# Halved value steps behind a modelled instruction store, tables of rules per stretch, and bulk transfers in pieces, in a four-layer attention kernel

## The chip, the cores and the metric

The program runs on one core of a Trainium2 chip. A core has five engines that run side by side and meet only at semaphores: TensorE (PE, matmuls; its weight loads are shown apart as PEld), ScalarE (ACT), VectorE (DVE), GpSimd (POOL) and SyncE (SP, which here only issues transfers). The metric is the device time of one execution in microseconds (us), median of several runs.

## The reference

The input is 2048 tokens of 512 numbers, with 32 heads of 16. Four residual blocks follow each other: A, B, A, B, with the same weights in both A and in both B.

```python
def A(x, wqkv, wo):                       # softmax attention
    q, k, v = heads(x @ wqkv)
    p = softmax(einsum("bhqd,bhkd->bhqk", q, k) * 16 ** -0.5)
    return merge(einsum("bhqk,bhkd->bhqd", p, v)) @ wo

def B(x, wqkv, w_phi, wo):                # linear attention, learned feature map
    q, k, v = heads(x @ wqkv)
    phi = lambda t: concat(softmax(t @ w_phi), softmax(-t @ w_phi))
    kv, z = phi(k).T @ v, phi(k).sum(0)
    return merge(phi(q) @ kv / (phi(q) @ z + 1e-6)) @ wo

for block in (A, B, A, B):
    x = x + block(layernorm(x))
```

An A block needs 32 x 2048 x 2048 exponentials, and that is where most of the time lies.

## The kernel before

**Tiles.** An A block (class LayerA) works on 32 groups: a group G is four heads and 512 queries. Within a group it goes over 16 steps kt of 128 keys, and each step has two halves of 128 x 1024 scores. So a block has 32 x 16 x 2 = 1024 score tiles. Three things happen to a tile:

- a *score step* on TensorE (`scores`, `score_cols`, L1266): 8 loads of weights and 8 matmuls of 512 columns in 16-bit numbers, into one of two PSUM tiles `s`;
- the exponential on ScalarE (L1273), from `s` to one of six SBUF tiles `p`;
- a *value step* on TensorE (`pvs`, L1316), one for the two tiles of a step kt: 8 matmuls of 512 columns in the program, in 32-bit numbers. Each of these stands in the trace as two matmuls and two weight loads. They sum into an accumulator, a pair of PSUM banks named `double` or `pm`.

A few tiles do not go through ScalarE: for them `power_task` forms the exponential by a polynomial on VectorE (L1284 to L1304), from a score step into `double` or `pm` to the one tile `px`. They are called *power tiles* below.

**Fillers.** Between these steps TensorE gets the rest of the block as *filler steps*: the projections of the next heads and the output projection (`mm_cols`, L713, 8 matmuls of 512 columns in 16-bit numbers, the shape of a score step), the transposes at the end of a block (L1386), and in the first block the turns and folds of block B's weights (`prep_b`, L438 and L446). They come from generators that yield ("pe", planned time).

**What sets the order.** `attention` is a planner that runs when the program is built. It keeps a modelled time for TensorE (`pe`), ScalarE (`act`) and the other engines, and writes the instructions down in the order that it finds. The engines follow that order on the chip and wait for semaphores only. In each turn it takes a score step if one of the two `s` tiles is free by then (`free`, from the start of the exponential before the last one, plus BACK), else a filler or a value step, if it is planned to end by the time the next score step is due. A value step may run over that time by LATE = 0.2 us. The planned prices are UNIT 0.217 us for a score or filler step, STEP 0.864 for a value step, EXP 0.904 for an exponential, 0.66 for a turn, a fold or a group of transposes. EAGER sets from which step on power tiles are taken although a filler waits: never in the first A block, always in the second.

**Blocks B** follow their own planners (`feed`, `flow`), with the same tables before and after.

**Transfers.** All bulk transfers are issued on SP, in the order of the program: an instruction that waits for a semaphore holds back everything behind it. Weights of block B are prepared during the first A block and go through DRAM (`split_parts`, `load_hl`, `begin`), as do parts of the attention output (`load_ob`, L1324).

## Time and profile before

| | |
|---|---|
| median of 3 runs | 2498.81 us (2496.61, 2498.81, 2501.56) |
| the profiled execution | 2493.94 us, span 2492.2 us |
| granted TensorE clock, mean | 0.989 |
| ScalarE busy | 2136.6 us, 86% of the span |
| TensorE busy | 2303.5 us, 92% |
| exponentials on ScalarE (L1273) | 2001, from 71.0 to 1008.3 us and from 1311.7 to 2238.8 us |

The two stretches in the last row are the A blocks; blocks B and the preparation lie around them. Times in rows of the profile are us from the start of the span. In rows of a timeline the columns are start, duration, engine, source line, operation, output and inputs, shape, and the number of instructions merged into the row; in brackets stands idle time of the engine before it and what ended it. The lines L are those of the kernel before, except in rows that are said to be of the changed one.

### The profile page before, as it was taken

The numbers are of one execution on the slowest core, as the hardware profiler recorded it, in microseconds if no ns is written. First come the engines' busy times: TensorE is split into PE (matmuls) and PEld (weight loads), VectorE is DVE, ScalarE is ACT, GpSimd is POOL, SyncE is SP. The second block draws the span as 40 slices with busy tenths as digits, with TensorE's granted clock in tenths as the row PEclk, the third lists the DMA queues.
The fourth block names the chain that finished last, engine by engine and source line by source line (L and its number), as shares of the span: only waits on it lengthen the run. The fifth ranks groups of instructions, "written<-read, shape, count | busy, mean of one in ns | idle before, by whom it ended". The sixth has DMA issues, their size and how long they took to land.

```text
span 2492.2 us, 103433 instructions
## 1 busy us (share of the span) xinstructions
PE 2303.5 (92%) x46698; PEld 1083.9 (43%) x46698; DVE 1602.2 (64%) x2866; ACT 2136.6 (86%) x2379; POOL 530.6 (21%) x644
## 2 busy tenths in 40 slices
PE   6999999999989999899889999999999999998998
PEld 4444444444434443445344444444443444444543
DVE  8233456756667455889973666667567652469897
ACT  6899999999999999444539999999999999993553
POOL 3111111121110000356441112111111000005553
PEclk9999999999999999999899999999999999999999
DMA  5412240132045331100124004203300441120003
GB/s 195 69 27 44 49 82 20 43 48 50 3 104 126 118 112 62 52 35 18 61 72 77 19 7 63 34 3 51 65 4 15 88 128 48 66 70 26 26 1 112
DMA packets 114925, 142.86 MB, mean 57 GB/s; under 512 B 64184, under 2 KB 69928, under 8 KB 112168
## 3 DMA queue, kind: packets, MB, share of 16 engines
q1 hardware_dynamic: 113288, 133.38, 21.7%
q8 instruction: 367, 6.01, 1.0%
q0 software_dynamic: 1184, 2.77, 0.3%
q14 instruction: 86, 0.70, 0.1%
HBM read 62.16 MB, written 41.94 MB: 42 GB/s over the span
## 4 chain that ended last, share of the span: by engine, by line
ACT 58%; PE 14%; issue 12%; DVE 12%; POOL 2%; DMA 0%; ACTq 0%; POOLq 0%; SPq 0%; DVEq 0%
ACT p L1273 57%; PE double L1316 3%; PE s L1266 2%; DVE su L1691 1%; PE pbv L1618 1%; PE pk L1618 1%; PE pq L1618 1%; PE pm L713 1%; DVE yt L1908 1%; DVE f L1683 1%; POOL f L1700 1%; DVE f L1684 1%; PE fl L1950 1%; DVE mx L1680 1%; PE pm L1316 1%
## 5 line engine op out<-in xcount | busy, mean ns | idle before, releaser
L1273 ACT ACTIVATE p<-s 128x1024 f32<-128x1024 f32 x2001 | 1853.0, 1063 | 19.2 <-PE s L1266 15.2
L1266 PE MATMUL s<-kq 49*32 49x512 f16 x15136 | 789.7, 381 | 102.7 <-ACT p L1273 86.8
L1266 PEld LDWEIGHTS <-kq 49*32 49x32 f16 x15872 | 385.8, 89 | 881.8 <-issue 795.9
L1316 PE MATMUL double<-p,v 64*32 64x512 f32 x9064 | 612.7, 591 | 0.0
L1316 PE MATMUL pm<-p,v 64*32 64x512 f32 x6944 | 475.6, 589 | 0.0
L977 POOL TENSOR_TENSOR yt<-yt,yt 128x512 f32<-128x512 f32 x64 | 84.8, 1324 | 764.1 <-DVE yt L974 742.3
L1316 PEld LDWEIGHTS double<-p,v 64*32 64x32 f32 x9064 | 174.1, 106 | 30.9 <-issue 6.2
L1618 PEld LDWEIGHTS <-xnTa 128*128 128x128 f16 x1152 | 111.1, 99 | 155.1 <-DVE f L1684 26.4
L1350 DVE SCALAR_TENSOR_TENSOR xt<-pm,c_oA,xt 128x512 f32<-128x512 f32 x102 | 76.2, 747 | 155.9 <-PE pm L713 151.9
L1097 POOL TENSOR_TENSOR sq<-stg 128x512 bf16<-128x512 f16 x48 | 57.7, 1202 | 478.1 <-DVE stg L1005 250.6
L1316 PEld LDWEIGHTS pm<-p,v 64*32 64x32 f32 x6944 | 135.0, 106 | 21.6 <-issue 2.6
L1700 POOL TENSOR_TENSOR f<-f,su 128x1024 f32<-128x1024 f32 x58 | 112.2, 1934 | 116.3 <-DVE su L1694 103.4
L974 DVE STREAM_TRANSPOSE yt<-double 128x512 f32<-128x512 f32 x72 | 47.3, 695 | 112.3 <-PE double L1316 112.1
L1618 PE MATMUL pbv<-wbv,xnTa 128*128 128x512 f16 x384 | 93.9, 397 | 21.7 <-DVE f L1684 21.7
L1685 ACT ACTIVATE f<-f,c_pB 128x1024 f32<-128x1024 f32 x62 | 70.4, 1148 | 49.6 <-DVE f L1684 42.3
L1706 ACT ACTIVATE fk<-f 128x1024 f16<-128x1024 f32 x30 | 31.7, 1057 | 74.7 <-POOL f L1700 74.7
L713 PEld LDWEIGHTS <-wA 64*32 64x32 f16 x4608 | 75.9, 93 | 44.8 <-issue 9.2
L974 DVE STREAM_TRANSPOSE yt<-pm 128x512 f32<-128x512 f32 x56 | 36.8, 696 | 90.4 <-PE pm L1316 90.1
L1000 DVE TENSOR_SCALAR tq<-double,c_qk 128x512 f32<-128x512 f32 x28 | 21.0, 749 | 108.0 <-PE double L713 101.0
L1618 PE MATMUL pq<-wbqk,xnTa 128*128 128x512 f16 x384 | 88.4, 379 | 0.7 <-DVE vt L1645 0.7
L1618 PE MATMUL pk<-wbqk,xnTa 128*128 128x512 f16 x384 | 88.1, 379 | 0.0
L1950 PE MATMUL fl<-wbo,obB 128*128 128x512 f16 x312 | 76.7, 403 | 8.7 <-ACT raw L1902 3.6
(342 smaller groups left out, 3083.2 us busy)
## 6 DMA issues: line engine op xcount, KB each, us to landing
kq<-stg SPq DMA_DIRECT2D x168, 128.0 KB
xd<-xt SPq DMA_DIRECT2D x40, 512.0 KB
xt<-xd SPq DMA_DIRECT2D x40, 512.0 KB
v<-vyt SPq DMA_DIRECT2D x384, 16.0 KB
oD<-osp SPq DMA_DIRECT2D x24, 256.0 KB
ob<-oD SPq DMA_DIRECT2D x8, 768.0 KB
xt<-in_A_x_dram SPq DMA_DIRECT2D x8, 512.0 KB
wbqk<-dBqk SPq DMA_DIRECT2D x2, 2048.0 KB
```

The source lines that it names most:

```text
L713: nc.tensor.matmul(ps[h][c, :], w[r, c], x[r], start=(n == 0), stop=(n == of - 1), skip_group_check=True)
L974: nc.vector.transpose(ys[u].rearrange("p a b -> p (a b)"), ps[u])
L977: nc.gpsimd.tensor_tensor(ys[0], ys[0], ys[1], ALU.add)
L1097: nc.gpsimd.tensor_tensor(sq, hi, hi, ALU.mult)
L1266: nc.tensor.matmul(banks2[u][32 * c:32 * c + 32, :], self.side(g, half, 64 * u, 0, kt * P + 32 * c, 32), self.side(g, half, 64 * u, 1, j * ...
L1273: nc.scalar.activation(pt, s, AF.Exp, scale=EXPS)
L1316: nc.tensor.matmul(acc[h][32 * hh:32 * hh + 32, :], self.oct[o]["v"][r, x:x + 32], pt[r, hh % 2, :], start=(kt == 0), stop=(kt == NT - 1), ...
L1350: nc.vector.scalar_tensor_tensor(xt[:, u, :], ps[h], con["oA"], xt[:, u, :], op0=ALU.mult, op1=ALU.add)
L1618: nc.tensor.matmul(dst, xnT[:, a, c, t * P:(t + 1) * P], w(b, c), start=(i == 0 and c == 0), stop=(i == 2 and c == NC4 - 1))
L1685: nc.scalar.activation(f, f, AF.Exp, scale=con["pB"])
L1700: nc.gpsimd.tensor_tensor(f3, f3, self.part_sums(f3, slice(0, 64), factor), ALU.mult)
L1950: nc.tensor.matmul(ps2[:, u, :], obs[j][:, c, a, t * P:(t + 1) * P], wo[:, b, c, :], start=(c == 0 and i == 0), stop=(c == NC4 - 1 and i = ...
```

## The change

1. **Halves.** `pvs` can do the columns 0 to 255 or 256 to 511 alone. Where a whole value step does not fit the room before the next score step, the planner may issue the first half (planned price HALF = 0.434 us), and the second when that fits. A half has as many matmuls and weight loads as a whole step, each over half the columns.
2. **The gate.** A first half is taken only while a modelled store of TensorE's instructions is well filled (`line[1] >= LEVEL`). The store holds at most DEPTH = 300 instructions and fills at RATE = 60 per us. Each score or filler step takes 16 out of it and each value step, whole or half, 32. If the model runs empty, planned time passes.
3. **Tables.** RULES replaces EAGER and LATE. For each A block and each of 16 stretches of 32 steps it has three numbers: how readily power tiles are taken (0 never, 1 if no filler waits, 2 always), by how much a whole step or a second half may run over, and by how much a first half may.
4. **Prices.** A turn or a group of transposes is planned at 0.85 and a fold at 1.15 us (still fitted as 0.66), and an exponential that had to wait for its scores costs 0.016 more.
5. **Two conditions.** Tiles of a group whose keys are not loaded yet no longer hold back other steps, and a filler that wants a PSUM pair may take one before a new accumulator if both are free.
6. **Pieces.** `spread` issues a bulk transfer as several, each with a part of every partition's row: 8 for block B's query and key weights, 4 for 1 MB tables, 3 for a block of attention output, 2 for the value weights.

```diff
+HALF = 0.434
+AGAIN = 0.016
+TURN, FOLD = 0.85, 1.15
+DEPTH, RATE, LEVEL = 300.0, 60.0, 250.0
-EAGER = (100, 0)
-LATE = 0.2
+RULES = (((2, 0.05, 0.01), (2, 0.05, 0.05), (2, 0.15, 0.0), (2, 0.15, 0.2), (2, 0.15, 0.0), (1, 0.15, 0.0), (2, 0.02, 0.1), (1, 0.02, 0.0),
...
+    def spread(dst, src, n):
+        m = src.shape[1] // n
+        for i in range(n):
+            nc.sync.dma_start(dst[:, i * m:(i + 1) * m], src[:, i * m:(i + 1) * m])
...
-            nc.sync.dma_start(self.wqk, dBqk)
+            spread(self.wqk.rearrange("p a b c n -> p (a b c) n"), dBqk.rearrange("p a b c n -> p (a b c) n"), 8)
...
+            def fetch(n, now):
+                line[1] = min(DEPTH, line[1] + (now - line[0]) * RATE) - n
+                line[0] = now
+                if line[1] < 0.0:
+                    line[0], line[1] = now - line[1] / RATE, 0.0
+                return line[0]
...
-                        if not slots:
+                        if not slots or self.groups[tiles[0][0]][0] not in self.kq:
                             free = due = FAR
...
-                            act = start + EXP
+                            act = start + EXP + (AGAIN if start > act + 0.002 else 0.0)
...
-                            pe += UNIT
+                            pe = fetch(16, pe + UNIT)
...
-                                    if min(self.pfree) <= pe and not soon:
+                                    if min(self.pfree) <= pe and (not soon or max(self.pfree) <= pe):
...
-                            if (G in acc or min(self.pfree) <= pe) and pe + STEP <= max(due, free) + LATE:
+                            room = max(due, free) - pe
+                            late, short = RULES[self.li][self.now // 32][1:]
+                            if half is not None and HALF <= room + late:
+                                pvq.popleft()
+                                idx, banks2 = acc[G]
+                                self.pvs(G, kt, banks2, slice(256, 512))
+                                half, step = None, HALF
+                            elif half is None and (G in acc or min(self.pfree) <= pe) and (STEP <= room + late or kt and HALF <= room + short and line[1] >= LEVEL):
...
+                                if STEP > room + late:
+                                    self.pvs(G, kt, banks2, slice(0, 256))
+                                    half = kt
+                                    pe = fetch(32, pe + HALF)
+                                    plan.now = pe
+                                    break
...
-                        if turn == 0 and tiles and pxfree <= pe and (need is None or self.now >= EAGER[self.li]) and plan.clock["V"] <= pe + VBUSY:
+                        if turn == 0 and tiles and pxfree <= pe and (eager == 2 or eager and need is None) and plan.clock["V"] <= pe + VBUSY:
```

**What it moves, counted over the built programs.** Of the 1024 value steps of the two blocks, 214 are split (85 in the first block, 129 in the second, 77 of these between its exponentials 560 and 810); 810 stay whole. Power tiles are 50 and were 47 (20 and 27 before, 22 and 28 now), so 1998 exponentials stay on ScalarE and were 2001. In the program before there are 127 places where two whole value steps stand with one score step alone between them (64 and 63 by block); in the changed one there is 1. SP issues 966 transfers on the main path and issued 865.

TensorE in the second A block, near its exponential 1567 of the 2001, before. `s` are score tiles, `kq` their operands, `p` the exponentials, `v` the values:

```order
L1266 MATMUL s<-kq_0_37689 32x512
L1316 MATMUL double<-p,v_31625 32x512 x8
L1266 LDWEIGHTS kq_1_37690
L1266 MATMUL s<-kq_1_37690 32x512
...
L1316 MATMUL double<-p,v_31625 32x512 x8
L1266 LDWEIGHTS kq_0_37689
L1266 MATMUL s<-kq_0_37689 32x512
```

The same place of the changed program (its L1277 and L1327 are L1266 and L1316 before):

```order
L1277 MATMUL s<-kq_0_38658 32x512
L1327 MATMUL double<-p,v_32516 32x256 x8
L1277 LDWEIGHTS kq_1_38659
L1277 MATMUL s<-kq_1_38659 32x512
...
L1327 MATMUL double<-p,v_32516 32x256 x16
L1277 LDWEIGHTS kq_0_38658
L1277 MATMUL s<-kq_0_38658 32x512
...
L1327 MATMUL double<-p,v_32516 32x256 x8
L1277 LDWEIGHTS kq_1_38659
L1277 MATMUL s<-kq_1_38659 32x512
...
L1327 MATMUL double<-p,v_32516 32x512 x8
```

Before, a whole value step stands on either side of one score step. Now a half stands there, then two halves, then a half: the two steps kt are spread over three gaps between score steps.

TensorE at the start of the first A block, before (after four score steps with nothing between them comes a value step), and then changed:

```order
L1266 MATMUL s<-kq_1_596 32x512
L1316 MATMUL double<-p,v_162 32x512 x8
L1266 LDWEIGHTS kq_0_595
L1266 MATMUL s<-kq_0_595 32x512
...
L713 LDWEIGHTS wAv
```

```order
L1277 MATMUL s<-kq_1_596 32x512
L724 LDWEIGHTS wAv
L724 MATMUL double<-xnT_0_154,wAv 32x512
...
L1277 LDWEIGHTS kq_0_595
L1277 MATMUL s<-kq_0_595 32x512
...
L724 LDWEIGHTS wAv
L724 MATMUL double<-xnT_0_154,wAv 32x512
...
L1277 LDWEIGHTS kq_1_596
L1277 MATMUL s<-kq_1_596 32x512
```

Five filler steps (projections of the next heads' values) now stand between the second and the third score step, and three between the third and the fourth. The second A block starts in the same way.

SP in the first A block, where the weights of block B and a block of attention output are fetched, before and then changed:

```order
L372 DMA dBqk<-bhl_18670 128x4096
L1324 DMA ob_19670<-oD 128x3072
L1594 DMA wbqk<-dBqk 128x8192
L1354 DMA xd_3_112<-xt 128x2x512
L1337 DMA xt<-in_A_x_dram 128x2x512
```

```order
L169 DMA dBqk<-bhl_19007 128x1024 x2
L1348 DMA xt<-in_A_x_dram 128x2x512 x2
L169 DMA ob_20290<-oD 128x1024 x3
L169 DMA wbqk<-dBqk 128x1024 x8
L1365 DMA xd_3_112<-xt 128x2x512
```

Three transfers with 8, 6 and 16 KB for each partition have become rows of transfers with 2 KB for each partition.

More of the change, by code (lines that the diff above doesn't have):

```diff
@@ L457, in prep_rest @@
         for i in range(2):
-            nc.sync.dma_start(folded[i], dF[i])
+            spread(folded[i], dF[i], 4)
         yield LAND
@@ L1323, in load_ob @@
             self.fetched[j] = self.plan.now
-            nc.sync.dma_start(self.obs[j], oD[j])
+            spread(self.obs[j], oD[j], 3)
         def part(self, j):
@@ L1514, in attention @@
                     need = self.side_need()
+                    eager = RULES[self.li][self.now // 32][0]
                     ready = 0
@@ L1525, in attention @@
                                 if kind == "M":
-                                    soon = pvq and (NT - pvq[0][1] <= ALIGN * what[0] or pvq[0][0] not in acc)
-                                    if min(self.pfree) <= pe and not soon:
+                                    soon = pvq and (NT - pvq[0][1] <= ALIGN * what[0] or pvq[0][0] not in acc and self.groups[pvq[0][0]][0] in self.kq)
+                                    if min(self.pfree) <= pe and (not soon or max(self.pfree) <= pe):
                                         s.need, s.holds = None, True
                                         break
-                                elif pe + what[0] <= (free + SIDE if len(what) == 1 else max(due, free)):
-                                    plan.now = pe + what[0]
+                                elif pe + min(what[0], 0.66) <= (free + SIDE if len(what) == 1 else max(due, free)):
                                     s.need = None
-                                    pe += what[0]
+                                    pe = fetch(16, pe + what[0])
+                                    plan.now = pe
                                     self.stream_need(s)
```

37 lines of the change are left out of this document (21 added, 16 removed), and 3 rows, old and new, of the table RULES.

## The prediction

> **What bounds the kernel now.** I read the page first (busy shares, chain, groups), then the two A blocks as windows, then single places in the timeline of TensorE. The page:
>
> ```profile
> PE 2303.5 (92%) x46698; PEld 1083.9 (43%) x46698; DVE 1602.2 (64%) x2866; ACT 2136.6 (86%) x2379; POOL 530.6 (21%) x644
> ACT 58%; PE 14%; issue 12%; DVE 12%; POOL 2%; DMA 0%; ACTq 0%; POOLq 0%; SPq 0%; DVEq 0%
> L1273 ACT ACTIVATE p<-s 128x1024 f32<-128x1024 f32 x2001 | 1853.0, 1063 | 19.2 <-PE s L1266 15.2 <-ACT p L1273 0.3
> ```
>
> The chain of waits runs through ScalarE for 58% of the span, and the exponentials of L1273 fill 1853 us. Idle time of ScalarE before them is only 19.2 us, so by this row hardly anything is to be gained. But one exponential lasts 1063 ns while they follow each other faster than that: they overlap, and a late one still counts as busy. What matters is the distance from one to the next. Windows give it, with the two A blocks first, then a stretch of 100 us; the columns are the stretch, its length, then busy us and count on PE, PEld, DVE, ACT and POOL, the granted clock, the share of the DMA engines and GB/s:
>
> ```profile
> 71.00:1009.40 938.40, 886.80 (x21435) 407.48 (x21442) 512.92 (x952) 929.77 (x1004) 112.60 (x107) 1.00 0.27 64
> 1311.70:2239.90 928.20, 875.82 (x21351) 398.62 (x21358) 541.97 (x964) 923.19 (x997) 110.41 (x103) 1.00 0.23 49
> 130.00:230.00 100.00, 97.16 (x2456) 45.43 (x2451) 36.16 (x61) 99.93 (x109) 15.38 (x12) 1.00 0.09 20
> ```
>
> In the good stretch the pace is 99.93 / 109 = 0.917 us for each exponential. Over the blocks it is 938.4 / 1004 = 0.935 and 928.2 / 997 = 0.931. At 0.917 throughout, the blocks would take 920.7 and 914.2 us, so 17.7 + 14.0 = 31.7 us are lost to something that comes and goes. The fastest pace in sight is this row of ScalarE's timeline, four exponentials with three distances of (3.77 - 1.06) / 3 = 0.90:
>
> ```profile
> 1373.67 3.77 ACT L1273 ACTIVATE p<-s 128x1024 f32<-128x1024 f32 x4
> ```
>
> TensorE's timeline shows where a late exponential comes from. First a place with two whole value steps around one score step, then one with fillers alone:
>
> ```profile
> 1834.54 0.63 PE L713 MATMUL pm<-xnTb,wA 64*32 64x512 f16 x16
> 1835.24 0.41 PE L1266 MATMUL s<-kq 49*32 49x512 f16 x8
> 1835.45 1.05 PE L1316 MATMUL double<-p,v 64*32 64x512 f32 x16
> 1836.32 0.41 PE L1266 MATMUL s<-kq 49*32 49x512 f16 x8
> 1836.54 1.05 PE L1316 MATMUL double<-p,v 64*32 64x512 f32 x16
> 1837.39 0.41 PE L1266 MATMUL s<-kq 49*32 49x512 f16 x8
> ...
> 1374.10 0.84 PE L713 MATMUL pm<-xnTb,wA 64*32 64x512 f16 x24
> 1374.75 0.41 PE L1266 MATMUL s<-kq 49*32 49x512 f16 x8
> ```
>
> Score steps start at 1835.24, 1836.32 and 1837.39, so the distance is 1.08 and 1.07 us, with TensorE never idle: a score step takes 0.22 (1835.45 - 1835.24) and a value step 0.86. One such distance is caught up by the score step after a filler, which has room to spare. Two in a row are not: ScalarE gets its second tile 1.075 us after the first, 0.16 over the pace of 0.917. TensorE has time enough in all (its value steps could be spread), but a piece of 0.86 does not fit between two score steps that should start every 0.9 us.
>
> **The change part by part.**
>
> *Value steps.* The order holds 127 places where two whole value steps stand around a lone score step, and 1 after the change. So 126 of these delays go, by 126 x 0.158 (1.075 - 0.917) = 19.9 us. Ends: with the blocks' mean pace of 0.933 in place of 0.917, 126 x 0.142 = 17.9; with the fastest pace of 0.90, 126 x 0.175 = 22.0. I take 19.9, since the gaps that replace them look like the stretch at 130 us, where single value steps alternate with short work.
>
> What comes in their place are halves. No row shows a value step over 256 columns. Below it lies the filler step: 24 matmuls take 1374.75 - 1374.10 = 0.65, so 8 take 0.217, and a half has 16 matmuls and 16 loads of the same width, 0.43. Above it lies the whole step with as many instructions, 0.86. I take 0.43: fillers already run as many instructions in that time. Gaps with a half (0.22 + 0.43) or a half and a filler (0.87) stay under the pace, even two halves in a gap (1.08) come seldom (36) and with a short gap on either side. So the 428 halves cost TensorE nothing that ScalarE sees; what hides them is its spare 0.917 - 0.22 in each gap. At 0.65 for a half, the 153 gaps that hold a half and something more would each run over by about 0.2.
>
> *Power tiles.* 47 become 50: 3 exponentials fewer on ScalarE, 3 x 0.917 = 2.8 us. Their work on VectorE lies beside the rest (542 of 928 us busy in the second block).
>
> *Gaps that are too full.* In the second block the new order has two gaps with three fillers and a whole value step (1.51 us of work) and two with a whole step and a half (1.29). With the score step that makes distances of 1.73 and 1.51, over the pace by 0.8 and 0.6: 2 x (0.8 + 0.6) = 2.8 us. Lower end 0, if ScalarE waits there for a free `p` anyway; I take 2.5, loss.
>
> *Starts.* At the start of a block TensorE's clock is low, which the planner's prices do not know:
>
> ```profile
> 1311.13 1.30 PE L1266 MATMUL s<-kq 49*32 49x512 f16 x16 [3.79 <-DMA kq<-sh]
> 1312.78 0.63 PE L1266 MATMUL s<-kq 49*32 49x512 f16 x8 [0.34 <-ACT p L1273]
> 1313.69 0.63 PE L1266 MATMUL s<-kq 49*32 49x512 f16 x8 [0.29 <-ACT p L1273]
> 1314.07 1.96 PE L1316 MATMUL double<-p,v 64*32 64x512 f32 x16
> 1315.78 0.68 PE L1266 MATMUL s<-kq 49*32 49x512 f16 x8
> ...
> 1314.00:1316.00 2.00, 2.00 (x32) 0.61 (x24) 0.00 (x0) 1.47 (x2) 0.00 (x0) 0.50 0.24 53
> ```
>
> The clock is 0.50, and a value step takes 1.71 (1315.78 - 1314.07). Five fillers before the third score step would take 5 x 0.43 = 2.2 us there, and ScalarE waits about 1.4 longer for its third tile than now. Against that, the fillers keep TensorE busy in the 0.34 + 0.29 us that it now waits, so the clock may come back sooner, and the late value step that costs a whole distance now may run at full speed. Ends -1 and +2 us for each block; I take 0 for both.
>
> *Store and pieces.* The instructions of TensorE arrive as transfers: 6.01 MB in 367 packets are 16.4 KB each, and 6.01 MB over 2 x 46698 matmuls and loads are 64 B each, so a packet brings 256. Four times in the A blocks TensorE stands still with nothing to wait for:
>
> ```profile
> q8 instruction: 367, 6.01, 1.0%
> ...
> 348.62 0.82 PE L713 MATMUL double<-xnT,wA 64*32 64x512 f16 x19 [0.61 <-issue]
> ...
> 817.10 0.63 PE L713 MATMUL pm<-woA,ob 64*32 64x512 f16 x16
> 819.22 0.41 PE L1266 MATMUL s<-kq 49*32 49x512 f16 x8 [1.50 <-ACT p L1273]
> ...
> 819.22 0.11 PEld L1266 LDWEIGHTS <-kq 49*32 49x32 f16 x8 [1.99 <-issue]
> ...
> 1565.87 0.62 PE L713 MATMUL double<-xnTb,wAv 64*32 64x512 f16 x15 [0.39 <-issue]
> ...
> 1799.64 0.61 PE L713 MATMUL pm<-xnTb,wA 64*32 64x512 f16 x12 [0.19 <-issue]
> ...
> 810.57 0.34 SPq L372 DMA_DIRECT2D dBqk<-bhl  x1
> 811.01 0.38 SPq L1324 DMA_DIRECT2D ob<-oD  x1
> 815.39 0.32 SPq L1594 DMA_DIRECT2D wbqk<-dBqk  x1
> ```
>
> In the row at 819.22 the wait is put down to ScalarE, but the loads beside it say "issue": no instruction was there. That is the longest, 1.50, and it follows three bulk transfers within 5 us. All four are 2.7 us of TensorE. Pieces of 2 KB for each partition may let the instruction packets through sooner: gain 0 to 2.7. The splits add 214 x 32 = 6848 instructions to 93396, 7.3%. Where they are densest (77 splits in 250 exponentials of the second block, some 229 us) that is 10.8 per us on top of 45 (4511 matmuls and loads in the row below), while the transfers of keys, which are not cut, take half of the DMA engines:
>
> ```profile
> 1930.00:2030.00 100.00, 93.72 (x2263) 42.27 (x2248) 64.03 (x105) 99.40 (x108) 7.71 (x6) 1.00 0.53 124
> ```
>
> A store that lasted just long enough at 45 per us runs dry at 56: loss 0 to 6, by up to nine stalls of the mean 0.67. I take 0 for both sides together, with ends -2.7 and +6. The Trainium skill ("Runtime: NRT & Kernel Launch", section Instruction fetch mechanics) agrees with the 16 KB and says that fetching the next block is mostly hidden behind the current one; the four stalls above are against "always". By its rule alone this term would be 0 on both sides and the slower rival below void.
>
> The pieces themselves cost SP 101 issues at 0.32 to 0.38, some 35 us spread over 2492. SP's queue holds later transfers back by 7 x 0.35 = 2.5 us at `wbqk`, which is issued at 815 and first read here:
>
> ```profile
> 1010.81 1.47 PE L1618 MATMUL pk<-wbqk,xnTa 128*128 128x512 f16 x6
> ```
>
> That cover is 195 us; if it were gone, the first projection of block B would wait by as much. The blocks of attention output are planned 14 us and more ahead of their use. The Trainium skill ("DMA: Bandwidth & Descriptors", section Rules for kernel authors) asks for 1 MiB and more in a transfer, which speaks against pieces of 256 KB; the row at 1010.81 says that nothing waits for them, so its rule changes nothing here.
>
> *The rest.* The prices for turns, folds and late exponentials move only the planner's own clock. A fold really takes longer than its planned 0.66:
>
> ```profile
> 276.45 1.16 PE L446 MATMUL pm<-phi,bwt 128*128 128x128 f32 x8
> 277.54 0.41 PE L1266 MATMUL s<-kq 49*32 49x512 f16 x8
> ```
>
> It is 1.09 from start to start. But it is still fitted as 0.66, and its eight places keep their delay: 0. The ends of both A blocks read alike in the two orders, and blocks B are untouched: 0.
>
> Sum: -19.9 - 2.8 + 2.5 + 0 + 0 = -20.2 us. The profiled execution took 2493.94 us (span 2492.2), so it would take 2473.7. It is 4.9 us below the median of the three runs, 2498.81; on that median the forecast is 2478.6, taken as 2478. A measurement can tell 0.2%, 5 us, from no change. The forecast's own range by the ends: best -22.0 - 2.8 + 0 - 2 - 2.7 = -29.5, worst -17.9 - 2.8 + 2.8 + 4 + 6 = -7.9, so 2469 to 2491.
>
> **The rivals.**
>
> *Half given back.* The delays of 1.075 go, but other things (clock at the starts, stalls, halves of 0.5 in the fullest gaps) sit at their bad ends and take 8 to 13 us. For it: the ends above are not remote, and all were priced from other shapes. Against it: they are independent. Time 2487 to 2493; the forecast proper is 2469 to 2487.
>
> *The delay moves.* A half costs 0.65, from loads that do not hide behind matmuls of half the length: 153 gaps of a half and more run over by 0.2, 30.6 us, against the 22.7 gained; with part of this caught up by the short gaps beside them the time is 2494 to 2504, no change. Against it: the filler rows run the same number of instructions in 0.217. The weight loads of `v` differ from those of fillers in one point, 106 against 93 ns in the profile's groups:
>
> ```profile
> L1316 PEld LDWEIGHTS double<-p,v 64*32 64x32 f32 x9064 | 174.1, 106 | 30.9 <-issue 6.2 <-ACT p L1273 0.5
> L713 PEld LDWEIGHTS <-wA 64*32 64x32 f16 x4608 | 75.9, 93 | 44.8 <-issue 9.2 <-DVE nm L1022 0.4
> ```
>
> *Slower: the store runs dry.* The place is the second block from 1830 to 2060, where halves and key transfers meet. At 56 instructions per us 229 us hold 50 packets. If each came late by as much as the worst one (1.50), that is 75 us, and 2554; it decides from 30 stalls of the mean 0.67 (20.2 us) up. With 40 to 50 such stalls the time is 2505 to 2512. Against it: there are 4 in the two blocks now, and the gate asks for a well filled store, if its model is right.
>
> That the change does not do what it says is out for the halves, which stand in the order; for the pieces it is the 0 to 2.7 above.
>
> **How the numbers follow.** Forecast 0.65, half given back 0.15, the delay moves 0.10, slower 0.07, and 0.03 for more than 29 us faster, from places that I have not seen. Faster by over 0.2% (under 2493.8) holds the forecast, the rival that gives half back and the last: 0.83; within 0.2%: 0.10; slower: 0.07. The predicted time is that of the likeliest case, 2478. The range of 2468 to 2492 takes in the ends worked out above with one us on either side; it holds the forecast and most of the second case, 0.8 of the chance.
>
> **What would show it.** In the windows of the A blocks: 1002 and 996 exponentials at a pace of 0.92 or less, about 10 us shorter each. In TensorE's groups: L1327 in two shapes, the one with 256 columns 6848 times, and two score steps around a half 0.65 or more apart with an idle gap, not 1.07. Distances of two value steps around one score step: 1. Waits by "issue" in the A blocks: near 817 none, between 1830 and 2060 a few. The forecast is wrong if a half takes over 0.5 us between starts, if those waits sum to more than 5 us, or if the starts of the blocks lose more than 2 us each.

## The result, and the profile after

| | before | changed |
|---|---|---|
| median of 6 runs, side by side | 2497.71 us (2495.50 to 2501.56) | 2478.32 us (2475.77 to 2482.57) |
| ratio of the two, 95% interval | | 0.9923 (0.9910 to 0.9936) |
| the profiled execution, and its span | 2493.94 us, 2492.2 | 2481.00 us, 2479.1 |

The change takes off 19.4 us; 20.2 was forecast, so the total was hit. The parts of the sum were not. The two profiled executions differ by only 12.9 us: before's lies 3.8 below its median, the changed one's 2.7 above, and the runs of the two kernels spread over 6.1 and 6.8 us.

The page of the changed kernel, with the lines that answer to those of before:

```profile
PE 2307.3 (93%) x50122; PEld 1149.3 (46%) x50122; DVE 1640.5 (66%) x2914; ACT 2121.8 (86%) x2376; POOL 531.3 (21%) x644
q8 instruction: 394, 6.46, 1.1%
L1284 ACT ACTIVATE p<-s 128x1024 f32<-128x1024 f32 x1998 | 1838.3, 1077 | 25.1 <-PE s L1277 23.6
```

Three exponentials fewer, 3424 matmuls more on TensorE, and 394 instruction packets in place of 367. Windows over the two A blocks and the stretch at 130 us:

```profile
70.97:1006.20 935.23, 891.46 (x22803) 437.61 (x22811) 540.44 (x1000) 922.22 (x1002) 113.05 (x107) 1.00 0.28 65
1306.08:2228.50 922.42, 878.29 (x23408) 434.45 (x23409) 556.78 (x979) 916.01 (x996) 111.21 (x103) 1.00 0.23 50
130.00:230.00 100.00, 94.85 (x2480) 46.04 (x2472) 68.51 (x112) 98.66 (x108) 13.52 (x11) 1.00 0.09 20
```

The blocks are 3 and 6 us shorter (938.40 and 928.20 before), the pace 0.933 and 0.926, not 0.92 or less. TensorE's timeline at a place where value steps are split:

```profile
1000.19 0.62 PE L1327 MATMUL pm<-p,v 64*32 64x256 f32 x16
1000.70 0.41 PE L1277 MATMUL s<-kq 49*32 49x512 f16 x8
1000.91 1.06 PE L1327 MATMUL pm<-p,v 64*32 64x256 f32 x32
1001.77 0.41 PE L1277 MATMUL s<-kq 49*32 49x512 f16 x8
1002.00 0.63 PE L1327 MATMUL pm<-p,v 64*32 64x256 f32 x16
1002.53 0.41 PE L1277 MATMUL s<-kq 49*32 49x512 f16 x8
```

Two halves take 1001.77 - 1000.91 = 0.86, so one takes 0.43. Score steps around one half are 0.76 apart (1001.77 to 1002.53), around two halves 1.07.

Where the time of the A blocks goes shows when the distances between the starts of exponentials are sorted. For each class the table gives their number in both blocks, and by how much they exceed 0.904 us in all. The last two columns are the first two experiments below.

| distance | before | changed | pieces alone | changed, uncut |
|---|---|---|---|---|
| under 0.96 | 1806, 15.4 | 1908, 20.4 | 1820, 16.4 | 1920, 21.4 |
| 0.96 to 1.1 (before, mostly two whole value steps around a score step) | 162, 26.0 | 51, 5.9 | 155, 25.0 | 45, 5.1 |
| over 1.1 | 31, 15.8 | 37, 24.7 | 24, 18.2 | 31, 27.0 |
| sum | 57.2 | 51.0 | 59.6 | 53.5 |

The middle class holds the forecast's 126 delays: set against TensorE's steps in the trace, 120 of its 162 distances before (20.5 us) follow two whole value steps around one score step, as does 1 of the 51 after. The class lost 20.1 us, close to the 19.9 worked out, though that was 126 times 0.158 and this is 111 distances fewer. But the ordinary distances exceed 0.904 by 5.0 more in sum (0.9 of this because 102 more belong to the class), and the long ones by 8.9 more. With 2.7 for three exponentials the blocks gain 20.1 - 5.0 - 8.9 + 2.7 = 8.9; the other 4.1 of the profiled difference lie behind the blocks.

What the long class gained is standstills of TensorE for want of instructions: the distances that hold one exceed 0.904 by 12.0 us in sum, and did so by 3.3 before. TensorE's waits by issue in the first A block (three rows), then in the second (two); the columns are us in all, times, longest:

```profile
PE pm L1327 <- issue: 2.8, 2, 2.6
PE s L1277 <- issue: 1.2, 3, 0.5
PE double L724 <- issue: 0.9, 1, 0.9
...
PE pm L724 <- issue: 2.0, 2, 1.4
PE s L1277 <- issue: 0.9, 2, 0.6
```

That is 7.8 us; before showed 0.6 + 1.50 in the first block and 1.0 in the second. The largest in the timeline, then windows around it:

```profile
799.18 1.04 PE L1327 MATMUL pm<-p,v 64*32 64x512 f32 x8
802.77 0.63 PE L1327 MATMUL pm<-p,v 64*32 64x512 f32 x4 [2.55 <-issue]
```

```profile
796.00:800.00 4.00, 4.00 (x100) 1.68 (x95) 1.31 (x2) 3.95 (x5) 1.11 (x1) 1.00 0.94 312
800.00:802.00 2.00, 0.22 (x4) 0.00 (x0) 0.85 (x3) 0.74 (x1) 0.16 (x1) 1.00 1.05 397
802.00:804.00 2.00, 1.23 (x25) 0.72 (x29) 0.00 (x0) 0.00 (x0) 0.00 (x0) 0.86 0.70 218
804.00:806.00 2.00, 2.00 (x45) 1.84 (x42) 0.00 (x0) 1.11 (x2) 0.00 (x0) 0.50 1.05 398
```

TensorE stops in the middle of a value step while the DMA engines are full (share 0.94, then 1.05, 397 GB/s). The last row shows the second price: the granted clock falls to 0.50. ScalarE's distance across the standstill (799.68 to 804.63) is 4.95 us, 4.05 over 0.904. The other standstills of this profile stand after the same sign: in the 4 us ahead of each of its ten waits by issue the DMA share is 0.73 to 1.03, against 0.28 and 0.23 over the blocks.

That these waits are for instructions can be read from their places. A packet brings 256 instructions. Counted over TensorE's matmuls and loads, the waits by issue of 0.2 us and more in the fourteen profiles of this text, from 70 to 2260 us, are 127, and 126 of them stand at the same place of a packet (remainder 193 or 194 of 256), as does the 1.50 before; of the 206 other waits of that length in the changed kernel 3 do. Each of the 126 ends 1.2 to 1.8 us after a packet on the instruction queue has been transferred. In the changed kernel's blocks such a transfer starts, by the median, 213 instructions before TensorE gets to the first one that it brings; ahead of the six waits over 0.5 us it started with 0 to 70 to go.

### The profile page after: what moved, and what is told of

Its sections match the earlier page's. It is cut to its first block, busy times and chain, and to the rows that moved or that the text cites. A ratio compares the mean times of both kernels' runs of the same rounds, so it can differ in the third digit from the quotient of the medians.

```text
span 2479.1 us, 110386 instructions
## 1 busy us (share of the span) xinstructions
PE 2307.3 (93%) x50122; PEld 1149.3 (46%) x50122; DVE 1640.5 (66%) x2914; ACT 2121.8 (86%) x2376; POOL 531.3 (21%) x644
## 4 chain that ended last, share of the span: by engine, by line
ACT 56%; PE 15%; DVE 13%; issue 12%; POOL 2%; SPq 1%; DMA 1%; POOLq 0%; ACTq 0%; DVEq 0%
ACT p L1284 55%; PE s L1277 3%; PE pm L1327 3%; PE double L1327 1%; PE pbv L1655 1%; DVE su L1728 1%; PE pk L1655 1%; DVE yt L1945 1%; PE pq L1655 1%; PE double L724 1%; DVE f L1720 1%; POOL f L1737 1%; DVE f L1721 1%; SPq L999 1%; DVE mx L1717 1%
## 5 line engine op out<-in xcount | busy, mean ns | idle before, releaser
L1277 PE MATMUL s<-kq 49*32 49x512 f16 x15104 | 793.4, 382 | 81.4 <-ACT p L1284 61.5
L1327 PE MATMUL pm<-p,v 64*32 64x512 f32 (+1 forms) x13216 | 805.5, 534 | 2.8 <-issue 2.8
L1277 PEld LDWEIGHTS <-kq 49*32 49x32 f16 x15872 | 388.8, 89 | 804.4 <-issue 704.8
L1327 PE MATMUL double<-p,v 64*32 64x512 f32 (+1 forms) x5848 | 320.6, 491 | 0.0
L1327 PEld LDWEIGHTS pm<-p,v 64*32 64x32 f32 x13216 | 262.2, 106 | 42.9 <-issue 7.3
L985 DVE STREAM_TRANSPOSE yt<-pm 128x512 f32<-128x512 f32 x92 | 60.5, 695 | 207.4 <-PE pm L1327 207.4
L1108 POOL TENSOR_TENSOR sq<-stg 128x512 bf16<-128x512 f16 x48 | 57.2, 1192 | 427.0 <-PE s L1277 266.3
L1327 PEld LDWEIGHTS double<-p,v 64*32 64x32 f32 x5848 | 116.5, 106 | 21.1 <-issue 3.2
L1011 DVE TENSOR_SCALAR tq<-double,c_qk 128x512 f32<-128x512 f32 x36 | 26.8, 745 | 116.0 <-PE double L724 111.3
L1361 DVE SCALAR_TENSOR_TENSOR xt<-pm,c_oA,xt 128x512 f32<-128x512 f32 x56 | 41.8, 746 | 80.5 <-PE pm L724 78.1
L985 DVE STREAM_TRANSPOSE vyt<-double 128x512 f32<-128x512 f32 x48 | 31.5, 692 | 87.9 <-PE double L724 84.7
L1361 DVE SCALAR_TENSOR_TENSOR xt<-double,c_oA,xt 128x512 f32<-128x512 f32 x56 | 41.8, 746 | 68.2 <-PE double L724 67.6
```

What stands on the lines that cost most here:

```text
L985: nc.vector.transpose(ys[u].rearrange("p a b -> p (a b)"), ps[u])
L1108: nc.gpsimd.tensor_tensor(sq, hi, hi, ALU.mult)
L1277: nc.tensor.matmul(banks2[u][32 * c:32 * c + 32, :], self.side(g, half, 64 * u, 0, kt * P + 32 * c, 32), self.side(g, half, 64 * u, 1, j * ...
L1327: nc.tensor.matmul(acc[h][32 * hh:32 * hh + 32, part], self.oct[o]["v"][r, x:x + 32], pt[r, hh % 2, part], start=(kt == 0), stop=(kt == NT ...
L1361: nc.vector.scalar_tensor_tensor(xt[:, u, :], ps[h], con["oA"], xt[:, u, :], op0=ALU.mult, op1=ALU.add)
```

## The experiments

Each kernel ran beside the kernel before on the same chip; its ratio goes by those runs.

**Pieces alone.** The kernel before, with `spread` at the places of part 6 of the change.

> The kernel before with the bulk transfers in pieces and nothing else; the order on TensorE is that of before. Theory (the gain lies in the split value steps, pieces are worth nothing): 2497.7 us, the same as before within 2 us. Rival (pieces let the instruction packets through): the stall of 1.50 us at 817 and part of the other three (2.7 us in all) vanish with what ScalarE loses after them, 2491 to 2495, and the waits of TensorE by issue in the A blocks fall from 2.8 us to under 1.

Measured: 2491.76 us, ratio 0.9983 (0.9975 to 0.9992), 4.2 us faster. In time the theory falls and the rival holds: pieces are worth 4 us with the old order. Where they gain it is not shown. The profiled run is the slowest of the eleven (2499.06 us); its blocks are together 2 us longer than before's, with a wait of 2.2 us for VectorE at 577. The wait of 1.50 near 817 is gone, but the waits by issue sum to 1.8 us (before 3.1), not to under 1, and the distances that hold them went only from 3.3 to 2.3 us.

**The changed kernel, uncut.**

```diff
     def spread(dst, src, n):
+        n = 1
```

> The changed kernel with every bulk transfer in one piece, as before; the order on TensorE is that of the changed kernel. Theory (pieces worth nothing): 2478 us within 2. Rival (pieces hold the instruction store filled, and the halves need that): 2484 to 2492, with waits by issue of 10 us and more in the A blocks instead of the 7.0 of the changed kernel.

Measured: 2486.91 us, ratio 0.9968 (0.9956 to 0.9980); the rival holds. The intervals of this kernel and of the changed one do not overlap: by the ratios the new order alone is worth 8.0 us, and order and pieces together 19.2. In the table its middle class is as small as the changed kernel's; the difference is not there. Its waits by issue in the second block, in a profiled run that is the fastest of its six:

```profile
PE s L1278 <- issue: 4.6, 5, 1.4
PE double L1328 <- issue: 1.3, 1, 1.3
PE pm L1328 <- issue: 0.8, 1, 0.8
PE pm L725 <- issue: 0.7, 1, 0.7
```

That is 7.4 us against 2.9, and 12.0 against 7.8 in both blocks. Six of these waits, 6.4 us, lie from 1923 to 2006, in the stretch from 1830 to 2060 where the rival with the dry store put the danger; the changed kernel has one of 0.6 there. The distances that hold waits by issue exceed 0.904 by 16.9 us, against 12.0, so these two profiles show 5 us of the 8.6 between the medians; their spans are only 1.7 us apart. So the denser stream of the new order asks for instructions faster than they come where the DMA engines are full, and pieces mend part of that. Pieces alone (4.2) and order alone (8.0) make 12.2; together they give 19.2. The surplus of 7 has an uncertainty of about 5 by the three intervals.

**More load on the DMA engines.** At 12 places of the second block 2 MB are copied in DRAM, with nobody waiting for them; in the first kernel in rows of 8 KB, in the second in rows of 2 KB.

```diff
                 nc.sync.dma_start(oD[j][:, o], dst)
+                if self.li == 1:
+                    pile(j + o == 0, dst, 1)
...
+    def pile(first, dst, n):
...
+        nc.sync.dma_start(src[0:1].rearrange("p (a n) -> p a n", a=4)[:, :, 0:128], dst[0:1, 0].rearrange("p (a n) -> p a n", a=4))
+        for i in range(2):
+            spread(tc.dram_tile([P, 4224], F16, name="sink")[:, 0:4096], src, n)
```

The second kernel has 4 in place of the 1, the number of pieces.

> The changed kernel with extra transfers that nothing waits for: at 12 places of the second A block (after each stored part of attention output) 2 MB are copied from DRAM to DRAM as two transfers with rows of 8 KB. The order on TensorE is that of the changed kernel. Theory (instructions come late where data transfers fill the DMA engines): a pile of 2 MB at the 397 GB/s of the fullest stretch fills the engines for 5 us or more, about as long as 256 instructions last at 52 per us, so nearly each pile delays a packet or two; at 0.5 to 2.5 us of standstill each 6 to 30 us more, 2484 to 2508, with waits by issue in the second A block of 8 us and more (2.6 in the changed kernel). Rival (the stalls come from dense halves, whatever the DMA engines do): 2478 to 2482 and no more waits by issue.

> The same extra copies at the same places, each of the two transfers in four pieces with rows of 2 KB: the same bytes, four times as many packets. Theory (a long packet of data ahead of the instruction packet is what costs; pieces mend that): clearly less than with rows of 8 KB, half of its loss or less. Rival (only the bytes count, the engines are full either way): the same loss as with rows of 8 KB, within 3 us; the pieces then help for another reason, such as the order on the queue.

Measured: 2510.69 us, ratio 1.0048 (1.0032 to 1.0065), and 2502.37, ratio 1.0026 (1.0013 to 1.0039); 32 and 24 us over the changed kernel, on TensorE's same order. The first is 3 us above the theory's range. The four largest waits by issue in the second block with rows of 8 KB, then with 2 KB:

```profile
PE s L1288 <- issue: 10.3, 5, 3.4
PE double L733 <- issue: 2.4, 3, 1.2
PE double L1338 <- issue: 2.2, 3, 1.7
PE pm L1338 <- issue: 1.5, 1, 1.5
```

```profile
PE s L1288 <- issue: 4.8, 6, 2.3
PE double L733 <- issue: 1.4, 2, 0.9
PE pm L733 <- issue: 1.3, 1, 1.3
PE double L1338 <- issue: 0.8, 1, 0.8
```

With the smaller rows that are left out they sum to 16.7 and 8.8 us, against 2.9. That data transfers make TensorE's instructions late is shown by this, and that pieces halve the waits as well. In time they save a quarter, neither half as the theory expected nor nothing as its rival did, and the two intervals overlap slightly; what the rest of the 24 us is (transfers of values and keys that queue behind the copies, the clock after a standstill) was not taken apart.

**Keys cut too.** The transfers of keys that have all 2048 columns go in halves of 1024.

```diff
-                q.dma_start(t[r:r + 16], src[:, 1:3, :])
...
+                n = sl.stop - sl.start
+                for b in ((slice(0, n // 2), slice(n // 2, n)) if n == S else (slice(0, n),)):
+                    q.dma_start(t[r:r + 16, :, b], src[:, 1:3, b])
...
```

> The changed kernel, with the transfers of the keys cut too: rows of 2 KB in place of 4 KB, 24 transfers for a pair of heads in place of 12. In the profile of the changed kernel the standstills at 311, 779, 1780 and 1785 (3.1 us in all) come while these transfers fill the engines, at 107 to 120 GB/s. Theory (shorter packets let instructions through): those standstills shrink to under 1 us, 2472 to 2477. Rival (a cut row costs as much as a whole one, so the keys take twice as long and land late): 2480 to 2500, with waits of score steps for DMA.

Measured: 2478.22 us, ratio 0.9929 (0.9915 to 0.9943), the changed kernel's time. In its profile no standstill is left at 311, 779 and 1780, but others stand at 606, 1383 and 1935; the sum in both blocks is 5.9 us (7.8 in the changed kernel). Neither the gain nor the loss can be told.

**No halves.** `LEVEL = 1e9`, so that no first half is taken.

> The changed kernel with its tables, prices and pieces, but no half is ever taken. In its order two whole value steps around one score step stand in 46 places (127 before, 1 in the changed kernel), 48 power tiles, and 58 gaps hold over 1.0 us of work between two score steps, most of them a whole step and a filler or power score (1 such gap before). Theory (each such place costs what the distances of the trace say): 81 places fewer give 81 x 0.158 = 12.8 us, one power tile more 0.9, and 57 distances of 1.30 in place of 0.917 take back 57 x 0.38 = 21.8, so about 2506, from 2498 to 2510. Rival (the stricter tables alone bring the gain, halves are an ornament): 2478 to 2486.

Measured: 2517.89 us, ratio 1.0087 (1.0074 to 1.0100). The rival falls clearly: the tables without halves cost 22 us against before. It is also 12 slower than the theory's figure and outside its range, from waits that it did not know. The longest:

```profile
PE pm L724 <- DVE pw L1298: 6.7, 2, 5.9
```

Here a filler waits for VectorE to finish a power tile, with the next score steps behind it. ScalarE's distances at this wait and at one of 2.1 us near 812 are 8.71 and 6.21 us, 13.1 over 0.904, about as much as the theory missed. The whole loss lies inside the blocks; the stretches behind them are 1.1 and 0.7 us shorter than before.

**One number for all stretches.**

```diff
-RULES = (((2, 0.05, 0.01), (2, 0.05, 0.05), (2, 0.15, 0.0), ...
+RULES = (((1, 0.05, 0.0),) * 3 + ((2, 0.05, 0.0),) * 13, ((2, 0.05, 0.0),) * 16)
```

(The first 3 and 13 answer to `EAGER = (100, 0)`: in the first block power tiles pass waiting fillers from step 100 of 512 on. The section on the kernel before says "never in the first A block", which is wrong.)

> The changed kernel with halves, gate, prices and pieces, but in place of the tables one number for both blocks: a whole step or a second half may run over by 0.05 us, a first half not at all; power tiles as in the kernel before (47). Its order has 151 split steps instead of 214, 1 place of two whole steps around one score step, 3 gaps over 1.0 us (6 in the changed kernel). Theory (halves do it, the table adds only its 3 power tiles, 2.8 us, and loses 2.5 in its four overfull gaps): 2478 within 3 us, and less than 7 us of waits by issue, since 2016 instructions fewer are fetched. Rival (the numbers of the table carry the gain): 2486 to 2496.

Measured: 2517.88 us, ratio 1.0084 (1.0071 to 1.0097), far outside the ranges of theory and rival. Windows from the last exponential of each block on, of the changed kernel and then of this one:

```profile
1006.15:1306.08 299.93, 265.64 (x1972) 136.53 (x1964) 265.64 (x444) 134.67 (x177) 156.60 (x254) 0.97 0.14 43
2228.52:2479.10 250.58, 223.80 (x1596) 108.30 (x1580) 220.11 (x348) 108.68 (x142) 125.27 (x125) 0.97 0.12 42
```

```profile
71.49:1007.33 935.84, 889.57 (x22737) 433.38 (x22741) 513.14 (x924) 924.08 (x1004) 113.27 (x107) 1.00 0.27 62
1007.33:1327.12 319.79, 273.95 (x2012) 140.12 (x2000) 284.75 (x488) 134.86 (x178) 156.56 (x254) 0.95 0.15 46
1327.12:2246.33 919.21, 874.70 (x22392) 420.71 (x22392) 531.97 (x935) 915.50 (x997) 111.21 (x103) 1.00 0.23 48
2246.33:2516.10 269.77, 232.42 (x1620) 111.95 (x1612) 232.59 (x377) 108.70 (x142) 125.26 (x125) 0.94 0.13 44
```

The A blocks are as short as the changed kernel's (935.8 and 919.2 against 935.2 and 922.4), with 63 splits fewer. The whole loss, 19.9 and 19.2 us, lies behind them. TensorE's timeline there:

```profile
1006.62 0.93 PE L721 MATMUL pm<-woA,osp 64*32 64x512 f16 x8
...
1022.29 1.50 PE L1394 MATMUL pm<-ident,xn 128*128 128x128 f32 x8
1034.39 0.61 PE L704 MATMUL po<-woA,osp 128*128 128x512 f16 x1 [10.60 <-DVE xnTa L611]
```

Six fillers of the output projection and three groups of transposes are left over when the exponentials end; in the changed kernel only one group of transposes is. Block B waits for the queries that they belong to (10.60 us in one piece).

**No gate.** `LEVEL = -1e9`.

> The changed kernel without the gate: a first half is taken whatever the modelled store holds. Its order has 85 splits in the first block, as the changed kernel, and 160 in the second (129), 992 instructions more; 1 gap over 1.0 us in the second block in place of 5; 48 power tiles in place of 50. Theory (the store is a real limit in the dense part): 31 splits more bring about 4 packets more in the second block, two to four standstills of 0.7 more, +1.4 to +2.8, two power tiles less +1.8, less the 2.5 of the overfull gaps: 2478 to 2481, waits by issue in the second block 4 to 6 us (2.6). Rival (the store runs dry without the gate): 2488 and more, with over 10 us of waits by issue there. Second rival (the gate does nothing): 2474 to 2478.

Measured: 2509.95 us, ratio 1.0053 (1.0039 to 1.0068), the time of the first rival but not for its reason: waits by issue of over 0.1 us in the second block sum to 0.4 (2.9 in the changed kernel). Its order too leaves six fillers of the projection behind the second block:

```profile
2236.26:2509.30 273.04, 232.13 (x1644) 111.76 (x1632) 237.90 (x393) 108.48 (x142) 125.26 (x125) 0.93 0.13 46
```

22.5 us of the loss stand in this row (250.58 in the changed kernel). In the timeline of its second block stands, besides:

```profile
1936.91 0.41 PE L1327 MATMUL pm<-px,v 64*32 64x256 f32 x2 [4.15 <-DVE px L1315]
```

There two halves wait for a power tile of VectorE. What the gate does to the store itself is left open: it changed the order, and the order changed the time.

**The old start.** The condition on PSUM pairs (the second part of point 5 of the change) is undone. With it goes the exception in `soon` for a group whose keys are not loaded.

```diff
-soon = pvq and (... or pvq[0][0] not in acc and self.groups[pvq[0][0]][0] in self.kq)
-if min(self.pfree) <= pe and (not soon or max(self.pfree) <= pe):
+soon = pvq and (... or pvq[0][0] not in acc)
+if min(self.pfree) <= pe and not soon:
```

> The changed kernel with the old condition on fillers: they may not take a PSUM pair before a new accumulator, so the block starts with a value step again instead of five fillers. Its order has 0 and 1 places of two whole value steps around one score step, 77 and 129 splits, 22 and 27 power tiles, all nearly as the changed kernel; but behind the last score step of the first block stand 6 filler steps of the output projection and three groups of transposes (one group in the changed kernel), as in the kernel with one number for the tables, where both blocks have this and the stretch from the first block's last exponential to the second block's first took 320.9 us instead of 301.0. Theory (what decides is whether the projection of the last queries is through when the exponentials end): 20 us more behind the first block and none behind the second, 2495 to 2502. Rival (the start of the block is what the condition touches, with ends of -1 to +2 us a block): 2475 to 2482.

Measured: 2521.82 us, ratio 1.0102 (1.0087 to 1.0117). The 20 us behind the first block and none behind the second came as the theory said:

```profile
70.40:1026.14 955.74, 892.68 (x22625) 430.96 (x22629) 530.98 (x957) 922.18 (x1002) 113.52 (x107) 0.99 0.26 61
1026.14:1345.82 319.68, 271.57 (x2019) 139.19 (x2008) 284.68 (x488) 134.80 (x177) 156.56 (x254) 0.95 0.15 46
2267.80:2517.30 249.50, 223.65 (x1596) 107.72 (x1580) 219.77 (x348) 108.49 (x141) 125.30 (x125) 0.97 0.12 42
```

But the first block itself is 20.5 us longer as well, which was not expected. Its longest hole in the timeline:

```profile
313.99 0.58 PE L1277 MATMUL s<-kq 49*32 49x512 f16 x1 [7.66 <-issue]
314.94 0.62 PE L1277 MATMUL s<-kq 49*32 49x512 f16 x7 [0.38 <-DMA kq<-sh]
```

Most of the 20.5 us is this hole and a lesser one at 550: score steps wait for keys whose projection or transfer came late. The 7.66 is put down to issue, but it is the one wait of the 127 that does not stand at the boundary of a packet; SP issued the transfers of these keys (`kq<-sh`) from 310.26 on, when TensorE already stood still, and the step behind waits for them. So the theory explains half of the loss. Whether the exception in `soon` made the keys late was not tried.

**Fewer splits, and weights spread in time.** A table with 79 splits in the second block; block B's query and key weights in eight pieces, each behind a small write of GpSimd 4 steps after the last; and both. The kernels with spread weights also hold back the load of block B's value weights (`bwv`) until step 400, behind such a write; it is issued at 793.9 instead of 791.3 us.

```diff
+        yield "until", lambda: a1.now >= 400
...
+        def piece(self, i):
...
+            nc.gpsimd.memset(dst[0:1, 2 * i, 0:1], 0.0)
+            nc.sync.dma_start(dst[:, 2 * i:2 * i + 2], src[:, 2 * i:2 * i + 2])
```

> The changed kernel with another table for the second block, under which 79 value steps are split there instead of 129 (1600 instructions fewer), with the same 1 place of two whole value steps around one score step, 3 gaps over 1.0 us (5), 27 power tiles (28) and the projection of the last queries through in time. Theory (each split costs about as much as its share of the standstills, 2.6 us over 129 in the profile of the changed kernel, so 50 are worth 1.0, and one power tile 0.9): 2476 to 2480, no difference that can be told. Rival (the splits themselves carry the gain): 50 x 0.16 = 8 us slower, 2484 to 2488.

> The changed kernel, in which each of the eight pieces of block B's query and key weights waits for a small write of GpSimd that the planner places 4 steps (7 us) after the one before, so that the pieces are spread over the last 120 us of the block instead of lying in one pile near 804; the order on TensorE is that of the changed kernel. Theory (piles of data transfers make instructions late): the longest standstill of the first block (2.55 us near 800, ScalarE loses 4) shrinks where the pile ends sooner, 2473 to 2477. Rival (the standstill at 800 comes from the transfers ahead of these weights, which stay as they are): 2477 to 2480 with the standstill in place. Second rival (SP waits and holds other transfers back): 2482 and more, with waits for DMA at the end of the block.

> The last two edits together: fewer splits in the second block and the spread weights. Theory: 2472 to 2477, the best of all kernels here if both help. Rival: 2477 to 2481, neither tells.

Measured: 2481.18 us, ratio 0.9941 (0.9928 to 0.9954); 2483.29, 0.9944 (0.9931 to 0.9957); 2482.25, 0.9942 (0.9929 to 0.9955). All intervals overlap the changed kernel's: no difference is shown, and none of the three beats it. Of their medians the first lies 1 us above its theory's range and the third 1 us above its rival's; the second lies in the range of its second rival (SP holding other transfers back), but TensorE has no wait for a transfer in the last 50 us of that block. The rival's 2484 to 2488 for fifty splits fewer is not reached, though the interval does not quite shut it out. Spreading the weights leaves the transfers ahead of them in place. In the profile of the second kernel the standstill near 803 is 0.30 us, but one of 1.69 ends at 600.8 (0.51 at that place in the changed kernel); in the third kernel 2.65 us stand at 801.7 again.

## Why the prediction was right, and where it was not

The total (2478 forecast, 2478.3 measured) came out and the range held. That it came within 0.3 us is luck: the forecast gave all of the gain to the order and none to the pieces, while the order alone measured 8.0 us of 19.2. Two terms were wrong, with opposite signs.

- **Value steps, -19.9.** Right for the delays themselves: of the 120 places found in the trace 1 is left, the class 0.96 to 1.1 lost 20.1 us, and a half costs 0.43. All 6848 matmuls over 256 columns run:

```profile
L1327 PE MATMUL pm<-p,v 64*32 64x256 f32 x3472 | 155.4, 377 | 0.0
L1327 PE MATMUL double<-p,v 64*32 64x256 f32 x2688 | 111.1, 375 | 0.0
L1327 PE MATMUL pm<-px,v 64*32 64x256 f32 x496 | 37.4, 375 | 0.0
L1327 PE MATMUL double<-px,v 64*32 64x256 f32 x192 | 14.7, 376 | 0.0
```

  But "the gaps that replace them look like the stretch at 130 us" was too good: the ordinary distances take 5.0 us back (0.9125 us each before, 0.9147 after). Why is open; halves are not needed for it, since the kernel without them has 0.9143 there.
- **Power tiles, -2.8.** The count fell by 3 as said. Their price alone was not tried.
- **Gaps that are too full, +2.5.** Distances of 1.73 us at 1855 and 1.59 at 1972 stand in the trace; the other two cannot be told from standstills beside them. Not refuted, not shown.
- **Starts, 0.** Within the ends, on the good side:

```profile
1306.22 2.51 PE L724 MATMUL double<-xnTb,wAv 64*32 64x512 f16 x40
1308.36 0.59 PE L1277 MATMUL s<-kq 49*32 49x512 f16 x8
1309.35 0.47 PE L1277 MATMUL s<-kq 49*32 49x512 f16 x8
```

  The five fillers take 2.1 us, and one distance between exponentials is 2.01; before there were three long ones, of 2.09, 1.28 and 1.57. That is 1.1 us won in the second block and 0.5 in the first.
- **Store and pieces, 0.** This is the step that failed. The relief was 4.2 us with the old order and, with the new one, 8.6 by the medians (2486.9 - 2478.3) or 11 by the ratios, beyond the end of 2.7. The forecast counted only standstills of TensorE in one profile (and four of 2.7 us; a fifth, of 0.38, stands at 1335), not the fallen clock after them, nor runs worse than the profiled one. Which of these makes up the difference is not shown. The new standstills, forecast as 0 to 6, came to 4.7 more by the profile (7.8 against 3.1). Two of the prediction's signs went against it: near 817 none was to stand, but the largest stands at 802, and 7.8 us of waits by issue are more than its 5.
- **The rest, 0.** The ends of the blocks do not read alike: before, two groups of transposes stand behind the first block's last score step, now one. The stretches behind the blocks are 2.4 and 1.7 us shorter in the profile. And what the tables, the gate and the condition at the start hold up was not seen: three experiments that changed one of them each lost some 20 us behind one block or behind both. The new prices (part 4 of the change) were not run alone.
- **The rivals.** "The delay moves" falls with the half of 0.43. "Half given back" comes closest for the new order without pieces (2486.9, forecast 2487 to 2493), but what gave time back there were the ordinary distances and the waits by issue, not the starts or slower halves. "The store runs dry" is the right mechanism at a small size: without pieces half of the waits by issue stand where it said, and it decides only with more load on the DMA engines (2510.7).

The Trainium skill ("Runtime: NRT & Kernel Launch", section Instruction fetch mechanics) calls the fetch of the next block mostly hidden; the waits by issue of 7.8 us agree with "mostly", and the 16.7 under the added copies show when it is not. The rule of 1 MiB and more in a transfer that the Trainium skill gives for the highest bandwidth ("DMA: Bandwidth & Descriptors", section Rules for kernel authors) would have kept the transfers whole; here cutting them won 4.2 us, so the measurement decides against it where nobody waits for the transfer.

## What to carry to other kernels

Where TensorE's instructions arrive through the same DMA engines as the data, look at the DMA share in the few us ahead of each wait by issue, and cut long bulk transfers that nobody waits for before making the instruction stream denser. In an order that a planner writes, check what is left over behind the last step of a stage: here six short steps left over cost 20 us, as much as all the delays that were removed. To tell a wait for instructions from another wait that the profile puts down to issue, see whether it stands at the boundary of an instruction packet. And an agreeing total proves no term; two edits made together have to be run apart.

## What the runs showed of the hardware

- A copy that no engine waits for slows TensorE through its instructions: 12 times 2 MB in one block raised its waits by issue from 2.9 to 16.7 us with rows of 8 KB and to 8.8 with rows of 2 KB.
- A standstill can cost more than its length: after 2.55 us without instructions the granted clock was 0.86, then 0.50 over 804 to 806, and ScalarE's distance across it was 4.95 us, 4.05 over 0.904.
- A value step over half the columns takes half the time (0.43 against 0.86) with as many matmuls and weight loads, so the loads do not bound the whole step.
- TensorE waits for its instructions at the boundaries of packets of 256: 126 of the 127 waits by issue of 0.2 us and more stand at one place of a packet, and end 1.2 to 1.8 us after a packet has been transferred.
